# Sharing out the elementwise steps of the first MoE anew, and spreading the first row block of w3 x w_out2 over four heads

## The chip, the cores and the metric

The kernel runs on one core of one Trainium2 chip. The metric is the device time of one execution in microseconds. Before the change it is 1256.09 us, the median of three runs (1256.04 to 1257.05). The profile comes from a further execution of 1256.72 us.

The engines are TensorE (PE in the profile; PEld is its weight load), VectorE (DVE), ScalarE (ACT), GpSimd (POOL) and SyncE (SP), whose queue issues the loads and nearly all stores. Each engine takes its instructions in a fixed order, and one that waits holds up all behind it.

## The reference

Attention over 4 batches of 12 heads, sequence 448, head size 64, with q and k normalized; then two blocks of matrix products on 1792 tokens of width 768:

```
scores = (1/8) * rmsnorm(q, g_q) @ rmsnorm(k, g_k).T
x = softmax(scores) @ v                     # per head; then [1792, 768]
x = relu(x @ w_in)**2 @ w_out               # w_in 768x2048, w_out 2048x768
a, b = x @ w1, x @ w2                       # 768x1024 each
out = ((a * b) @ w3) @ w_out2               # w3 1024x1024, w_out2 1024x768
```

q, k and v are float32; the weights come as 64-bit floats.

## The kernel before

**Precision.** Nearly every product is made from three matmuls (`mm3`, L256 to L260): each float32 operand is held as a high half, rounded to the type that the PE takes (`F32R`), and a low half, the remainder. Making the halves of a tile is a copy (high, `copy_on`, L104/L106/L108 by engine) and a subtraction (low, `sub_on`, L112; its line is the same on DVE and POOL, so the profile tells them apart by engine and tile).

**Weights.** They come in units of 128x384 or 128x512, listed in `units` in the order of their use. Units 0 to 31 are w3 and w_out2, units 32 to 119 (`U0` to `U1`) are w_in, w_out, w1 and w2 for the first batch, all as 64-bit floats. Such a unit takes these steps: the load (L178, SP) into one of four 64-bit buffers; `words`, which turns the high word on ACT (L192) and the low word, called the conversion here, on ACT (L195) or POOL (L197); `join` on DVE (L204), which puts both together into one of four float32 buffers; the high half on ACT (L104); the low half on DVE or POOL (L112, tile `hl`). Units of the first batch's MoE are also stored as float32 (L212), and the later batches load those. A join frees the 64-bit buffer for the load four units on, and the low half frees the float32 buffer for the join four units on. `LOW_ENG` says by the unit's number modulo its length where the conversion runs (g POOL, a ACT), `LO0_ENG` the same for the low half of the first 120 units (v DVE).

**Stages.** `w3o` is w3 x w_out2, computed once: 8 row blocks (`ic`) of 16 groups of three matmuls, 384 matmuls in all (`gen_w3o`). The first block uses w_out2 for the first time, so each of its groups brings one more unit of w_out2 in; the later blocks find the 16 units in place. It runs beside heads 0 to 12. The MoE of batch b (`gen_moe`) runs beside the twelve heads of batch b + 1 and the last alone; it holds 336 groups of three matmuls, 28 a head. Within it, half of w_in (16 units), half of w_out (12), the other halves, w1 and w2 (32 units), then w3o (12 float32 units).

**Order.** The loop over heads (L663) traces the stages of a head, and between them six calls of `fill(n)`, each of which takes matmul groups from the running generator until their yields, 3 for a group, have used up the credit n. For w3o, n is the total `W3O` over 78 calls (13 heads). The tile framework's planner then fixes each engine's order at build time: it starts from the order of tracing and moves an instruction ahead where, by its own estimates, its inputs and buffers are there first. So the order on an engine is near that of tracing, not the same.

**Attention, as far as it is touched.** `head_prep` splits k and q; q's high half is scaled on the engine of `QHI_ENG` by batch (a ACT, L487; v DVE, L489), its low half on DVE. `stage_qk` makes scores (L520, L521) and their maxima (L522, tile `nb`), `stage_exp` the exponentials (L538, tile `p`), `stage_t` their transposes (L560, tile `pt`), whose halves go to `ptr`. `stage_v` multiplies by v (L609) into a PSUM bank of the pool `ps_kv`, which has one, and DVE adds the two parts (L617, tile `xf`). For each pair of heads `norms_to_rows` transposes the softmax sums (L598) into that same bank, and DVE multiplies `xf` by them (L623). The pool `ps_mm`, with three banks, serves the products of w3o and the MoE.

`relu2` (L324) follows each product of w_in: ACT makes the relu and its square's high half, DVE the square (L330, tile `gf`), POOL the low half (L112, tile `act`).

Of the kernel before, what the change touches and what calls it, by code (L numbers as in the profile page):

```python
# [8 lines left out]
F32 = mybir.dt.float32  # L9
# [20 lines left out]
def attention_moe_kernel(  # L30
# [25 lines left out]
    NIC = w3t.shape[0] // 2  # L56
# [3 lines left out]

    LOW_ENG = "gga"
    LO0_ENG = "ggggv"
    KHI_ENG = "ggvv"
    KLO_ENG = "gvvv"
    QHI_ENG = "aavv"
    VLO_ENG = "gvgv"


    SPLIT_AHEAD = 2
    HI_AHEAD = 1
    JOIN_AHEAD = 2
    WORD_AHEAD = 3
# [65 lines left out]
    U0 = len(units)  # L140
# [23 lines left out]
    U1 = U0 + 2 * NFC + 4 * NE + 4 * NJ  # L164
    raws = {}
# [23 lines left out]
    def words(i):  # L189
        t, n = raws[i], units[i][0].shape[-1]  # L190
        hi = t[:, :n, 1].bitcast(F32)
        nc.scalar.activation(out=hi, in_=hi, func=AF.Prelu, scale=2.0**-112, alpha=-(2.0**32))  # L192
        low = t.rearrange("p n t -> p (n t)").bitcast(U16).rearrange("p (n t) -> p n t", t=4)[:, :n, 1]
        if LOW_ENG[i % len(LOW_ENG)] == "a":
            nc.scalar.activation(out=t[:, :n, 0], in_=low, func=AF.Copy, scale=2.0**-13, bias=2.0**-14 - 0.5)  # L195
        else:
            nc.gpsimd.tensor_scalar(  # L197
                out=t[:, :n, 0], in0=low, scalar1=2.0**-13, scalar2=2.0**-14 - 0.5, op0=ALU.mult, op1=ALU.add
            )
# [26 lines left out]
    def split_lo(i):  # L226
        n = units[i][0].shape[-1]
        t = hls[i]
        sub_on(LO0_ENG[i % len(LO0_ENG)] if i < U1 else "g", t[:, 1, :n], raws.pop(i)[:, :n], t[:, 0, :n].bitcast(F32))

    def upto(what, i, step):
        while pos[what] <= min(i, NU - 1):
# [35 lines left out]
    def gen_w3o():  # L268
        for ic in range(NIC):
            ws = None  # L270
            for half in range(2):
                ps = ps_mm.tile([128, 512], F32, name="mm", tag="mm")
                for jc in range(NIC):
                    if ws is None or jc * 2 // NIC >= len(ws):
                        ws = (ws or []) + [use(w3_at[2 * ic + len(ws or [])])]
                    if ic == 0:
                        advance(wo_at[half, jc])
                        wo[half, jc] = hls.pop(wo_at[half, jc])
                    w = ws[jc * 2 // NIC]
                    mm3(ps[:, :HC], w, jc % (NIC // 2), hl_pair(wo[half, jc], HC), jc, NIC)  # L280
                    yield 3
                o = t2.tile([128, S], F32, name="osb", tag="osb")
                copy_on("a", o[:, :HC], ps[:, :HC])
                k, c = divmod(ic, NIC // 2)
                nc.sync.dma_start(
                    out=w3o.rearrange("(e k) p (c m) -> e k p c m", k=2, m=128)[half * 3:half * 3 + 3, k, :, c, :]
                    .rearrange("e p m -> p e m"),
                    in_=o[:, :HC].rearrange("p (e m) -> p e m", m=128),
                )
# [26 lines left out]
    def gen_moe(b):  # L316
# [4 lines left out]
        for half in range(2):  # L321
            g = []

            def relu2(ps):  # L324
                r = t2.tile([128, S], F32, name="r", tag="r")
                nc.scalar.activation(out=r, in_=ps, func=AF.Relu)
                t = actp.tile([128, 2, S], F32R, name="act", tag="act")
                gf = t2.tile([128, S], F32, name="gf", tag="gf")
                nc.scalar.activation(out=t[:, 0, :], in_=r, func=AF.Square)
                nc.vector.tensor_tensor(out=gf, in0=ps, in1=r, op=ALU.mult)  # L330
                sub_on("g", t[:, 1, :], gf, t[:, 0, :].bitcast(F32))
                g.append(t)

            def keep(e):
                def f(ps):
                    acc[e] = accp.tile([128, S], F32, name="acc", tag="acc")
                    copy_on("a", acc[e], ps)
                return f

            def add(e):  # L340
                def f(ps):
                    nc.vector.tensor_tensor(out=acc[e], in0=ps, in1=acc[e], op=ALU.add)
                    t = x2p.tile([128, 2, S], F32R, name="x2", tag="x2")
                    copy_on("v", t[:, 0, :], acc[e])
                    sub_on("g", t[:, 1, :], acc[e], t[:, 0, :].bitcast(F32))
                    x2[e] = t
                return f

            yield from products(u, x, KX, [relu2] * (NFC // 2), half == 0)
            u += NFC  # L350
            yield from products(u, g, KF, [(add if half else keep)(e) for e in range(NE)])
            u += 2 * NE
# [240 lines left out]
    def norms_to_rows(h):  # L593

        rs = sums2.pop(h // 2)
        ps = ps_kv.tile([128, 512], F32, name="kv", tag="kv")
        for c in range(C):
            nc.tensor.transpose(ps[:, c * P:(c + 1) * P], rs[:, c, :], ident)  # L598
        return ps[:, :S]
# [43 lines left out]
                state["gen"] = None  # L643

    MOE = 3 * (NFC * KX + 2 * NE * KF + 2 * NJ * KX + NE * NIC)
    W3O = 3 * 2 * NIC * NIC

    nc.sync.dma_start(out=g_sb, in_=g_in)
    load_group(0)
# [105 lines left out]
```

## Time and profile before

| | us |
|---|---|
| median of the runs | 1256.09 |
| the profiled execution | 1256.72 |
| its span, first to last instruction | 1254.9 |
| PE busy | 1176.6 (94%) |
| POOL busy | 788.5 (63%) |
| ACT busy | 749.0 (60%) |
| DVE busy | 692.6 (55%) |

The busy shares are means over stages of different kinds. In the page's forty slices of 31 us PE stands at 3, 7 and 8 tenths in the first three, at 9 in the next four, at 7 to 9, mostly 8, from the eighth to the thirteenth, which lie in the first MoE, and at 9 from there on. DMA is at 6 to 8 tenths in the first MoE and at 3 or 4 after it. So the stages are to be read one by one: by their busy time, then by what PE and DVE wait for in them.

### The profile page before, as it was taken

What the parts mean: (1) busy time and instruction counts of PE and PEld (TensorE: products, weight loads), DVE (VectorE), ACT (ScalarE), POOL (GpSimd) and SP (SyncE); (2) the same over time, 40 slices, a digit from 0 to 9 for tenths busy, and PEclk for the clock granted to TensorE, in tenths of its full rate; (3) what the DMA queues carried; (4) which work ended last, traced back from release to release, by engine and by line L of the source; (5) the groups of instructions that cost most, each with busy time, mean ns of one, the idle gap of its engine ahead of it and who ended that gap; (6) DMA issues with size and microseconds to landing.
All of it is one profiled execution on the core that took longest, in us unless ns stands there. A gap on an engine that the chain in (4) does not pass through costs nothing.

```text
span 1254.9 us, 18695 instructions
## 1 busy us (share of the span) xinstructions
PE 1176.6 (94%) x6192; PEld 1063.9 (85%) x6192; DVE 692.6 (55%) x1274; ACT 749.0 (60%) x1595; POOL 788.5 (63%) x770
## 2 busy tenths in 40 slices
PE   3789999798888999999999999999999999999998
PEld 2578888687777889999999998999999999999998
DVE  6699877666668676556557546555664431012100
ACT  5788877776755665665655555655545554443342
POOL 5874427746765555675876664765765656768773
PEclk9899999998998989999999999999999999999999
DMA  7774447866866754433334344333433333433342
GB/s 211 243 222 135 150 143 205 260 199 192 257 171 200 229 154 143 123 111 115 114 92 124 96 130 137 96 105 86 117 89 88 92 106 110 120 104 111 101 122 94
DMA packets 102129, 178.71 MB, mean 142 GB/s; under 512 B 11056, under 2 KB 65552, under 8 KB 102032
## 3 DMA queue, kind: packets, MB, share of 16 engines
q1 hardware_dynamic: 98576, 172.01, 46.9%
q10 hardware_dynamic: 3456, 5.51, 1.2%
q8 instruction: 49, 0.80, 0.3%
q14 instruction: 48, 0.39, 0.1%
HBM read 149.95 MB, written 27.53 MB: 141 GB/s over the span
## 4 chain that ended last, share of the span: by engine, by line
PE 65%; DVE 5%; DMA 4%; POOL 3%; ACT 2%; issue 2%; SPq 0%; POOLq 0%; DVEq 0%; ACTq 0%
PE mm L258 18%; PE mm L259 18%; PE mm L260 18%; PE pt L560 3%; PE kv L609 3%; DMA raw<-w 2%; DVE raw L204 2%; POOL hl L112 2%; PE sc L520 2%; PE sc L521 2%; DMA raw<-w_in 1%; DVE nb L522 1%; PE kv L504 1%; PE kv L598 1%; ACT p L538 0%
## 5 line engine op out<-in xcount | busy, mean ns | idle before, releaser
L112 POOL TENSOR_TENSOR hl<-raw,hl 128x384 fp32r<-128x384 f32 (+1 forms) x395 | 459.3, 1166 | 270.3 <-ACT hl L104 266.8
L104 ACT ACTIVATE hl<-raw 128x384 fp32r<-128x384 f32 (+1 forms) x416 | 234.0, 564 | 147.2 <-PE mm L260 79.3
L259 PE MATMUL mm<-x,hl 128*128 128x448 f32 (+1 forms) x832 | 307.3, 369 | 7.8 <-POOL x L112 7.8
L258 PE MATMUL mm<-x,hl 128*128 128x448 f32 (+1 forms) x832 | 311.9, 375 | 2.8 <-ACT x L104 1.8
L260 PE MATMUL mm<-x,hl 128*128 128x448 f32 (+1 forms) x832 | 306.3, 368 | 2.0 <-POOL hl L112 1.2
L258 PE MATMUL mm<-act,hl 128*128 128x448 f32 (+1 forms) x640 | 239.0, 373 | 0.0
L259 PE MATMUL mm<-act,hl 128*128 128x448 f32 (+1 forms) x640 | 235.7, 368 | 3.0 <-POOL act L112 2.9
L260 PE MATMUL mm<-act,hl 128*128 128x448 f32 (+1 forms) x640 | 234.6, 367 | 1.6 <-DVE hl L112 1.4
L538 ACT ACTIVATE p<-sc,nb,rr 112x448 f32<-112x448 f32 x192 | 137.5, 720 | 82.3 <-DVE nb L523 81.8
L259 PEld LDWEIGHTS mm<-x,hl 128*128 128x128 f32 x832 | 158.9, 191 | 21.7 <-POOL x L112 9.5
L258 PEld LDWEIGHTS mm<-x,hl 128*128 128x128 f32 x832 | 158.8, 191 | 17.4 <-ACT x L104 3.2
L260 PEld LDWEIGHTS mm<-x,hl 128*128 128x128 f32 x832 | 158.7, 191 | 16.3 <-POOL hl L112 2.3
L204 DVE SCALAR_TENSOR_TENSOR raw<-raw 128x384 uint32<-128x384 uint32 (+1 forms) x120 | 94.9, 794 | 77.0 <-POOL hl L112 66.3
L259 PEld LDWEIGHTS mm<-act,hl 128*128 128x128 f32 x640 | 121.9, 191 | 14.2 <-POOL act L112 4.6
L522 DVE TENSOR_REDUCE nb<-sc 112x1 f32<-112x448 f32 x192 | 113.3, 616 | 35.3 <-PE sc L521 34.0
L260 PEld LDWEIGHTS mm<-act,hl 128*128 128x128 f32 x640 | 121.8, 190 | 11.9 <-DVE hl L112 1.8
L112 POOL TENSOR_TENSOR act<-gf,act 128x448 fp32r<-128x448 f32 x96 | 117.5, 1225 | 22.0 <-DVE gf L330 8.5
L258 PEld LDWEIGHTS mm<-act,hl 128*128 128x128 f32 x640 | 122.2, 191 | 9.4
L112 DVE TENSOR_TENSOR ptr<-pt,ptr 128x448 fp32r<-128x448 f32 x144 | 86.8, 618 | 72.2 <-ACT ptr L104 72.0
L560 PE MATMUL pt<-ident,p 112*128 112x112 f32 (+1 forms) x768 | 101.0, 269 | 13.1 <-DVE ptr L112 10.3
L192 ACT ACTIVATE raw<-raw 128x384 f32<-128x384 f32 (+1 forms) x120 | 71.4, 598 | 57.9 <-DMA raw<-w 25.5
L560 PEld LDWEIGHTS pt<-ident,p 112*128 112x128 f32 (+1 forms) x768 | 82.5, 138 | 20.4 <-DVE ptr L112 10.9
(76 smaller groups left out, 1517.5 us busy)
## 6 DMA issues: line engine op xcount, KB each, us to landing
raw<-f_in SPq DMA_DIRECT2D x96, 192.0 KB, 2.4
raw<-f_out SPq DMA_DIRECT2D x72, 256.0 KB, 2.6
raw<-f SPq DMA_DIRECT2D x96, 192.0 KB, 2.4
raw<-w_in SPq DMA_DIRECT2D x32, 384.0 KB, 3.5
raw<-w_out SPq DMA_DIRECT2D x24, 512.0 KB, 4.2
raw<-w SPq DMA_DIRECT2D x32, 384.0 KB, 3.8
raw<-w3o SPq DMA_DIRECT2D x48, 256.0 KB, 2.7
qt<-q_t SPq DMA_DIRECT2D x48, 224.0 KB, 2.8
```

The costliest lines, as they stand in the source:

```text
L104: nc.scalar.activation(out=out, in_=in_, func=AF.Copy)
L112: e.tensor_tensor(out=out, in0=in0, in1=in1, op=ALU.subtract)
L192: nc.scalar.activation(out=hi, in_=hi, func=AF.Prelu, scale=2.0**-112, alpha=-(2.0**32))
L204: nc.vector.scalar_tensor_tensor(out=f[:, :n].bitcast(U32), in0=t[:, :n, 1], scalar=3, in1=t[:, :n, 0], op0=ALU.logical_shift_left, op1=AL ...
L258: nc.tensor.matmul(ps, w[:, 0, wk, :], x[0], start=(i == 0), stop=False)
L259: nc.tensor.matmul(ps, w[:, 0, wk, :], x[1], start=False, stop=False)
L260: nc.tensor.matmul(ps, w[:, 1, wk, :], x[0], start=False, stop=(i == last))
L520: nc.tensor.matmul(o[j], d["qh"][:, c * P:(c + 1) * P], d["kt"], start=True, stop=False)
L522: nc.vector.tensor_reduce(out=nb[:, j:j + 1], in_=o[j], axis=AX.X, op=ALU.max, negate=True)
L538: nc.scalar.activation(out=p, in_=o[j], func=AF.Exp, scale=d["rq"][:, c:c + 1], bias=nb[:, j:j + 1], accum_out=sm[:, i, c:c + 1],)
L560: nc.tensor.transpose(ps[:kn, c * P:(c + 1) * P], d["p"][c][:, k0:k0 + kn], ident)
L609: nc.tensor.matmul(ps[:, :S], w, m, start=(n == 0), stop=(n == len(ops) - 1))
```

## The change

Six edits:

- The conversions of units 32 to 119 all run on POOL; before, every third was on ACT.
- The low halves of units 32 to 119 run on DVE for every third unit (g, g, v); before for every fifth. Units 0 to 31 keep both patterns.
- q's high half of the second batch's heads (12 to 23) is made on DVE instead of ACT.
- In the first MoE alone, the low half of the squared relu is made on DVE instead of POOL.
- The first row block of w3o asks 10.5 credits for a group instead of 3 (`FIRST = 3.5`), and `W3O`, from which n follows, grows to match: 3 x 2 x 8 x (8 + 2.5) = 504 instead of 384.
- `norms_to_rows` takes its PSUM tile from `ps_mm` instead of `ps_kv`.

```diff
-    LOW_ENG = "gga"
-    LO0_ENG = "ggggv"
+    LOW_ENG = ("gga", "g")
+    LO_ENG = ("ggggv", "ggv")
...
-    QHI_ENG = "aavv"
+    QHI_ENG = "avvv"
...
+    FIRST = 3.5
...
-        if LOW_ENG[i % len(LOW_ENG)] == "a":
+        low_eng = LOW_ENG[i >= U0]
+        if low_eng[i % len(low_eng)] == "a":
...
-        sub_on(LO0_ENG[i % len(LO0_ENG)] if i < U1 else "g", t[:, 1, :n], raws.pop(i)[:, :n], t[:, 0, :n].bitcast(F32))
+        lo_eng = LO_ENG[i >= U0]
+        sub_on(lo_eng[i % len(lo_eng)] if i < U1 else "g", t[:, 1, :n], raws.pop(i)[:, :n], t[:, 0, :n].bitcast(F32))
...
-                    yield 3
+                    yield 3 * FIRST if ic == 0 else 3
...
-                sub_on("g", t[:, 1, :], gf, t[:, 0, :].bitcast(F32))
+                sub_on("g" if b else "v", t[:, 1, :], gf, t[:, 0, :].bitcast(F32))
...
-        ps = ps_kv.tile([128, 512], F32, name="kv", tag="kv")
+        ps = ps_mm.tile([128, 512], F32, name="mm", tag="mm")
...
-    W3O = 3 * 2 * NIC * NIC
+    W3O = 3 * 2 * NIC * (NIC + FIRST - 1)
```

## Rows read from the trace of the kernel before

**Rows 1.** Busy time by stretches: us, then each engine's busy time, clock, DMA.

```profile
12.85:57.70 44.85, 28.13 (x100) 20.08 (x100) 30.26 (x63) 29.90 (x65) 35.96 (x38) 0.92 0.73 230
57.70:190.90 133.20, 121.50 (x744) 109.36 (x743) 115.90 (x238) 113.03 (x245) 66.20 (x81) 1.00 0.55 164
213.30:467.30 254.00, 220.65 (x1087) 194.15 (x1088) 172.52 (x300) 169.08 (x364) 156.24 (x161) 0.93 0.71 210
535.20:735.80 200.60, 200.60 (x1088) 184.10 (x1087) 120.95 (x213) 116.93 (x254) 137.49 (x129) 1.00 0.38 111
```

**Rows 2.** The same view for L520 alone: PE and PEld, clock, DMA.

```profile
213.30:467.30 254.00, 14.69 (x36) 6.47 (x37) 0.93 0.71 210
535.20:735.80 200.60, 13.10 (x36) 6.25 (x36) 1.00 0.38 111
```

**Rows 3.** Waits of PE, 213.3 to 467.3: total us, times, longest.

```profile
PE kv L598 <- DVE xf L617: 11.9, 4, 4.2
PE pt L560 <- DVE ptr L112: 9.2, 5, 3.5
PE sc L520 <- ACT p L538: 8.8, 8, 2.9
```

**Rows 4.** Waits of DVE, 213.3 to 467.3.

```profile
DVE raw L204 <- POOL hl L112: 60.2, 36, 3.3
```

**Rows 5.** The chain of waits, 401 to 409: start, us, what.

```profile
401.84 3.39 DMA raw<-w
...
405.38 0.53 POOL raw L197
...
405.99 1.03 POOL hl L112
...
407.04 1.36 DVE raw L204
...
408.42 3.54 DMA raw<-w
```

**Rows 6.** POOL in order of time: first 512-wide conversion and first 512-wide low half.

```profile
307.86 0.85 POOL L197 TENSOR_SCALAR raw<-raw 128x512 uint32<-128x512 uint16 x1
...
327.87 1.29 POOL L112 TENSOR_TENSOR hl<-raw,hl 128x512 fp32r<-128x512 f32 x1
```

**Rows 7.** The chain's shares by line, 213.3 to 467.3.

```profile
by line: DMA raw<-w 11.5%; DVE raw L204 9.2%; POOL hl L112 8.5%; issue 7.8%; DMA raw<-w_in 5.5%; DVE nb L522 3.8%; PE mm L258 3.7%; PE mm L259 3.7%; PE mm L260 3.6%; ACT p L538 2.4%; POOL act L112 2.3%; ACT hl L104 2.2%; POOL raw L197 2.0%;
```

**Rows 8.** Groups by line and form, POOL and DVE, 213.3 to 467.3.

```profile
L112 POOL TENSOR_TENSOR act<-gf,act 128x448 fp32r<-128x448 f32 x20 | 24.6, 1231 | 15.7 <-ACT act L104 6.4 <-DVE gf L330 5.1 <-ACT act L329 3.8
L197 POOL TENSOR_SCALAR raw<-raw 128x384 uint32<-128x384 uint16 x32 | 20.6, 644 | 39.9 <-DMA raw<-w 20.0 <-DMA raw<-w_in 10.7 <-DVE nb L522 4.5
L197 POOL TENSOR_SCALAR raw<-raw 128x512 uint32<-128x512 uint16 x16 | 12.8, 801 | 3.2 <-DMA raw<-w_out 2.0
...
L112 DVE TENSOR_TENSOR hl<-raw,hl 128x384 fp32r<-128x384 f32 x11 | 7.7, 696 | 2.0 <-ACT hl L104 2.0
```

**Rows 9.** Groups by line and form, DVE, 500 to 1020.

```profile
L489 DVE TENSOR_SCALAR qh<-qt,gg 128x448 fp32r<-128x448 f32 x22 | 10.4, 475 | 0.0
```

**Rows 10.** Busy time of L259 alone, one matmul a group, 12.85 to 92.7.

```profile
12.85:92.70 79.85, 18.21 (x46) 9.55 (x46) 0.96 0.73 223
```

**Rows 11.** PE in order of time: the first score matmul of head 4.

```profile
89.32 0.46 PE L520 MATMUL sc<-kt,qh 128*112 128x448 f32 x1 [1.19 <-ACT p L538]
```

**Rows 12.** PE in order of time: the same matmul of two groups in succession.

```profile
66.69 0.33 PE L259 MATMUL mm<-x,hl 128*128 128x384 f32 x1
...
67.21 0.33 PE L259 MATMUL mm<-x,hl 128*128 128x384 f32 x1
```

**Rows 13.** Waits of PE, 12.85 to 57.7.

```profile
PE mm L259 <- POOL x L112: 7.5, 4, 2.9
PE mm L259 <- POOL act L112: 2.9, 4, 1.3
```

**Rows 14.** The join's line: count, duration in ns (least, median, most), forms.

```profile
L204 DVE SCALAR_TENSOR_TENSOR raw<-raw x120: 500/679/1637, 11.4 to 458.6; 128x384 uint32<-128x384 uint32 x80, 128x512 uint32<-128x512 uint32 x40
```

## The prediction

> **What bounds the kernel now.** I began with the busy time of each engine by stretches, cut at the first score matmul (L520) of a head [rows 1]. Two stretches hold the same TensorE work: heads 14 to 22, which run beside the first MoE, and the corresponding nine heads beside the second one; each has 36 L520 matmuls [rows 2] and about 1088 matmuls in all. The second takes 200.6 us with PE busy throughout, the first 254.0 us with PE busy for 220.6 us and a mean granted clock of 0.93 of full speed. So 53.4 us are lost there: 33.3 us in which PE stood still, and roughly 254.0 x 0.07 = 18 us of half clock. All that follows head 22 runs at PE's pace, so what is gained or lost before it reaches the end one for one. The other place with slack is the start: PE is busy for 28.1 of 44.9 us in heads 0 and 1, but for 121.5 of 133.2 us in the rest of the w3 x w_out2 stretch.
>
> Next came the waits of PE in the slow stretch [rows 3]: it waits for attention results that DVE is late with, hardly ever for a weight tile. DVE's own waits explain that [rows 4]: 60.2 us, in 36 pieces, before the join (L204), all for the POOL subtraction that makes the low half of an earlier weight unit (I call it LO) and by that gives the f32 buffer back. Everything queued on DVE behind the join stands too.
>
> Then the chain of waits, to see why POOL is late [rows 5]. One round there: load of a unit 3.39 us, its low-word conversion on POOL 0.53, LO 1.03, join 1.36, next load; 408.42 - 401.84 = 6.58 us. LO does not need the load before it; it only stands behind that unit's conversion in POOL's queue. The timeline shows how far ahead [rows 6]: the first 512-wide conversion (unit 76) runs at 307.86, and six 384-wide LOs, five on POOL and one on DVE, come between it and the first 512-wide LO at 327.87. So the conversion of unit i+6 stands ahead of LO(i). LO(i) frees the buffer of join(i+4), which frees that of load(i+8), whose conversion stands ahead of LO(i+2): two units a round, 3.29 us a unit. PE wants a 384-wide unit every 22.3 / 9.33 = 2.39 us (28 groups of three matmuls a head, three groups a unit; 22.3 is a ninth of 200.6). Where the conversion stands only five ahead, three units share a round, 2.19 us each, which is no limit. That is what limits this stretch.
>
> **The change, part by part.** The first MoE has 88 units, numbers 32 to 119.
>
> LO. Before, i%5 = 4 puts 18 on DVE and 70 on POOL. After, i%3 = 2 puts 30 on DVE: 24 leave POOL, 12 come to it. A join waits no longer for POOL where LO has left; I take the 60.2 us [rows 4] in proportion: -60.2 x 24/70 + 60.2 x 12/70 = -10.3 us. Bounds: -20.6 (those that come cost nothing) and the slower rival's +8.8.
>
> The relu-square subtractions, 16 in all, leave POOL for DVE. POOL act pieces make up 2.3% of the chain through the stretch [rows 7], 5.8 us for 20 instructions, 13 of them these (the rest are the gated ones): -3.8 us. Bounds 0 and 16 x 1.231 = -19.7 us [rows 8].
>
> What DVE takes in return: 12 net LOs and 16 subtractions at 0.696 us and 12 q conversions (heads 12 to 23) at 0.475 us (a row of the later batches, where DVE does them already): 8.4 + 11.1 + 5.7 = 25.2 us [rows 8, 9]. DVE's named pieces are 9.2 + 3.8 = 13% of the chain, smaller ones come on top; I take 20%: +5.0 us. Bounds 0 and +25.2. The new subtraction also makes DVE wait for ScalarE's square; nb, ptr and xf queue behind it, and PE waits for those. ScalarE is relieved, so I put nothing more on it.
>
> Conversions. 30 (i%3 = 2; 22 narrow, 8 wide) go from ScalarE to POOL: 22 x 0.644 + 8 x 0.801 = 20.6 us more there. They hold 2.0% of the chain now, 5.1 us for 48; 30 more: +3.2 us. Bounds 0 and +20.6. ScalarE's relief I cost at zero: its join-feeding work waits for loads in any case. After the change every unit's conversion stands in POOL's queue, but the units whose conversions move are the ones with LO on DVE (both i%3 = 2, and six is a multiple of three), so the six-ahead order closes on no LO that it did not close on before, except for the 12 that come.
>
> The bank. The norm transposes (L598) take one of three mm banks in place of the one kv bank, so they no longer wait for the xf add: 11.9 us in four spells [rows 3]. Neither the transposes nor the xf add are among the chain's larger pieces [rows 7]: PE would mostly run into the next late DVE result (ptr, in the same rows as the spells). I take an eighth, -1.4 us; bounds -11.9 and, as an mm bank is now held until DVE has multiplied by it (L623), 18 x 0.7 = +12.6 us if each of the 18 pairs of heads from the first MoE on held a product up for one DVE operation of 0.7 us.
>
> The start. The credit of the first row block goes from 48 to 168, the total from 384 to 504; a head gives 6/78 of the total, so the block takes 168/38.8 = 4.3 heads instead of 48/29.5 = 1.6. A third of the way through head 4 is 92.7 us (it begins at 89.32 [rows 11]); in the trace 46 of 128 groups had begun by then [rows 10], where the credits give 43. With 16 by then, 30 groups go later, each 0.52 us [rows 12]: 15.6 us of PE. The early heads lose the waits for unit halves, 7.5 + 2.9 = 10.4 us [rows 13], and the moved work as far as PE was the last engine there, its busy share 28.1/44.9 = 0.63: 9.8 us. The later heads gain 15.6 us. -10.4 - 9.8 + 15.6 = -4.6 us. Bounds: -22.1 (all 26.0 us saved early, and 11.7 us of PE's idle time later take the work in but for 3.9) and +5.2 (only the waits go). Next late in the early heads are ScalarE and DVE with softmax.
>
> Sum: -10.3 - 3.8 + 5.0 + 3.2 - 1.4 - 4.6 = -11.9 us. The profiled execution took 1256.7 us, of which 1254.9 are span and 1.8 lie around it; that makes 1244.8 for it, and its 0.6 us above the median of the runs, 1256.1, taken off, 1244.2.
>
> A rule that speaks against the change: some joins last far longer than the shortest, 0.500 us against 0.679 in the middle and 1.637 at most [rows 14]. The Trainium skill ("SBUF — State Buffer", section "Who interferes with whom") says that a VectorE instruction with two SBUF inputs and a GpSimd instruction that reads SBUF exclude each other for the whole of whichever began first. The trace agrees as far as that spread goes, and the moved subtractions are of that kind. What it would make of the sum, worked out from the rows, is the first rival.
>
> **Rivals.** *Port.* Each of the 28 moved subtractions is held up as the longest join was, 1.637 - 0.500 = 1.14 us: 31.9 us more on DVE, x 0.2 = +6.4, 1250.6 us. For it: the spread of the joins; against it: the LOs on DVE averaged 0.696 us in the same stretch. *Three units a round.* With POOL's queue shorter and a third of LOs off it, two-unit rounds become rare; half of the 53.4 us goes, with the start -31.3, 1224.8 us. For it: 3.29 against 2.19 us a unit; against it: the other two residues keep their conversion six ahead. *Slower.* The 12 LOs that come to POOL now stand behind a conversion that waits for its load, as DVE's did not. Each of the 8 narrow ones turns a three-unit round into a two-unit round, 3.29 - 2.19 = 1.10 us, +8.8, while the 24 that leave had conversions of ScalarE ahead of them, were in three-unit rounds, and bring nothing: 8.8 in place of -10.3, 1263.3 us. The other terms together are -1.6 us, so the time turns to the slower side where the LO term passes +1.6. For it: the rounds; against it: the 24 that leave also no longer stand behind POOL's other subtractions. *No change*, the LO term zero: 1254.5 us. That the block isn't spread, because the planner pulls matmuls ahead of their credit, would cost the 4.6 us of the start; 46 groups begun against 43 credited says that it follows the credits.
>
> **How the numbers follow.** Forecast 0.40, port 0.10, three units 0.19, no change 0.12, slower 0.19. Faster by over 0.2% (about 2.5 us, which is what a measurement here can tell from no change) is the first three, 0.69; same 0.12; slower 0.19. Since cases of both signs weigh, the range reaches from below the large gain, 1222, to the slower case, 1264; about 0.08 lies outside at either end. The forecast's own range is 1238 to 1250.
>
> **What would show it.** Heads 14 to 22 at 245 to 248 us with PE's clock above 0.93; DVE's wait for POOL before the join near 50 us; POOL about 12 us less busy in the first MoE and DVE about 25 us more; L598 no longer waiting for the xf add; head 4 reached before 89.3 us and head 13 some 5 us before 190.9. The prediction is wrong if that wait stays at 60 us or moves to another releaser, if conversions stand further ahead than six, or if the first thirteen heads take longer than before.

## The result, and the profile after

The kernel after takes 1263.87 us (median of 4 runs, 1263.61 to 1265.94) against 1256.57 for the kernel before on the same chip: ratio 1.0055, interval 1.0038 to 1.0071, about 7 us slower. The forecast was 11.9 us faster. The profiled execution has a span of 1261.8 us, 6.9 above that of before.

Busy time by stretches of the kernel after, cut at the same score matmuls and with the same columns as [rows 1]: heads 0 and 1, heads 2 to 12, heads 14 to 22, and the nine heads beside the second MoE.

```profile
12.10:49.90 37.80, 22.94 (x82) 16.22 (x83) 24.88 (x58) 26.16 (x58) 27.39 (x30) 1.00 0.73 222
49.90:201.90 152.00, 132.92 (x760) 119.91 (x759) 122.26 (x252) 113.73 (x248) 79.53 (x93) 0.92 0.52 154
224.50:473.80 249.30, 216.57 (x1087) 188.75 (x1088) 188.65 (x331) 152.11 (x330) 149.43 (x159) 0.97 0.72 213
541.70:743.20 201.50, 201.07 (x1088) 184.17 (x1087) 120.92 (x213) 116.61 (x254) 137.86 (x129) 1.00 0.39 110
```

Against [rows 1]: heads 0 and 1 are 7.1 us shorter, heads 2 to 12 are 18.8 us longer, heads 14 to 22 are 4.7 us shorter, the last stretch agrees to a microsecond. Head 13 begins at 201.9 instead of 190.9. So the loss arises in the first thirteen heads, where 4.6 us were to be gained, and the first MoE gives a part back. What it gives back is not idle time: PE stands still for 32.7 us in heads 14 to 22 (249.30 less 216.57) against 33.3 before. PE is busy for 4.1 us less with the same matmuls, at a granted clock of 0.97 instead of 0.93.

Waits of PE in heads 14 to 22 after:

```profile
PE pt L564 <- DVE ptr L114: 13.2, 8, 3.4
PE sc L524 <- ACT p L542: 6.3, 9, 1.5
PE mm L264 <- POOL hl L114: 4.6, 3, 2.9
```

and the first row of DVE's:

```profile
DVE raw L207 <- POOL hl L114: 49.4, 29, 3.8
```

The norm transposes' wait [rows 3] is gone and the one for `ptr` grew from 9.2 to 13.2 us. DVE's wait before the join fell from 60.2 [rows 4] to 49.4 us; 50 were forecast. DVE is 16.1 us busier there, POOL 6.8 us less.

Groups by line and form after, POOL and DVE in the same heads:

```profile
L200 POOL TENSOR_SCALAR raw<-raw 128x384 uint32<-128x384 uint16 x48 | 33.3, 694 | 42.9 <-DMA raw<-w 18.8 <-DMA raw<-w_in 10.8 <-DVE raw L207 6.4
...
L200 POOL TENSOR_SCALAR raw<-raw 128x512 uint32<-128x512 uint16 x23 | 21.7, 945 | 20.7 <-DMA raw<-w_out 15.8 <-DVE vhl L114 2.2 <-DVE khl L114 2.0
```

```profile
L114 DVE TENSOR_TENSOR hl<-raw,hl 128x384 fp32r<-128x384 f32 x17 | 12.6, 743 | 0.4 <-ACT hl L106 0.2
L114 DVE TENSOR_TENSOR act<-gf,act 128x448 fp32r<-128x448 f32 x13 | 10.0, 767 | 0.1
```

A narrow conversion takes 0.694 us instead of 0.644, a wide one 0.945 instead of 0.801 [rows 8], and a low half on DVE 0.743 instead of 0.696.

Now the start. The same matmul line in head 2, and, from a second window, in head 5 (count, duration in ns: least, median, most):

```profile
L263 PE MATMUL mm<-x,hl x3: 444/522/687, 53.1 to 63.4; 128*128 128x384 f32 x3
...
L263 PE MATMUL mm<-x,hl x5: 334/335/422, 98.7 to 101.7; 128*128 128x384 f32 x5
```

Waits of PE before head 4 after, for the low halves of w_out2's units:

```profile
PE mm L263 <- POOL x L114: 13.6, 5, 4.7
...
PE mm L263 <- POOL act L114: 3.4, 2, 2.0
```

These were 10.4 us before [rows 13], were to vanish, and are 17.0. The halves themselves come later. POOL's low halves of the w_out2 units in the tiles `x`, first before, then after (count, duration in ns, first and last start):

```profile
L112 POOL TENSOR_TENSOR x<-raw,x x7: 993/1217/1847, 15.7 to 54.7; 128x384 fp32r<-128x384 f32 x7
...
L114 POOL TENSOR_TENSOR x<-raw,x x7: 998/1377/1849, 14.5 to 77.3; 128x384 fp32r<-128x384 f32 x7
```

The last of them begins 22.6 us later: `gen_w3o` advances a unit of w_out2 together with the group that first uses it, so spreading the groups spread the making of the halves too. Last, two stretches side by side: up to head 4, and heads 6 to 12. Before:

```profile
12.85:89.30 76.45, 54.13 (x252) 42.73 (x252) 59.97 (x115) 56.30 (x121) 60.30 (x64) 0.96 0.72 218
...
112.30:190.90 78.60, 74.65 (x463) 68.22 (x464) 64.14 (x142) 66.08 (x146) 31.76 (x45) 1.00 0.48 142
```

After, with heads 2 and 3 by themselves as a third row:

```profile
12.10:85.70 73.60, 48.17 (x184) 36.65 (x185) 51.50 (x108) 49.70 (x109) 51.54 (x57) 0.86 0.64 194
...
108.00:201.90 93.90, 86.95 (x528) 80.57 (x529) 76.79 (x169) 71.77 (x156) 42.66 (x54) 0.98 0.50 146
...
50.00:85.70 35.70, 25.13 (x104) 20.33 (x103) 26.62 (x50) 23.43 (x52) 24.15 (x27) 0.71 0.54 162
```

Up to head 4 PE has 68 matmuls less and is busy for 6.0 us less, but it stands idle for 25.4 us against 22.3. Heads 6 to 12 hold 65 matmuls more and last 15.3 us longer.

### The profile page after: what moved, and what is told of

Same layout as the page of the kernel before. It is cut to its first block, busy times and chain, and to the rows that moved or that the text cites. A ratio compares the mean times of both kernels' runs of the same rounds, so it can differ in the third digit from the quotient of the medians.

```text
span 1261.8 us, 18712 instructions
## 1 busy us (share of the span) xinstructions
PE 1179.1 (93%) x6192; PEld 1065.9 (84%) x6192; DVE 710.9 (56%) x1314; ACT 727.8 (58%) x1553; POOL 784.4 (62%) x772
## 4 chain that ended last, share of the span: by engine, by line
PE 66%; DVE 9%; DMA 8%; POOL 7%; ACT 5%; issue 4%; SPq 0%; POOLq 0%; DVEq 0%; ACTq 0%
PE mm L263 18%; PE mm L264 18%; PE mm L262 18%; PE pt L564 4%; PE kv L613 3%; POOL hl L114 3%; DMA raw<-w 2%; PE sc L524 2%; PE sc L525 2%; DVE raw L207 2%; DMA raw<-w_out 2%; ACT p L542 2%; DVE nb L526 2%; DMA qn<-q_nat 1%; POOL raw L200 1%
## 5 line engine op out<-in xcount | busy, mean ns | idle before, releaser
L114 POOL TENSOR_TENSOR hl<-raw,hl 128x384 fp32r<-128x384 f32 (+1 forms) x383 | 445.4, 1166 | 269.0 <-ACT hl L106 266.1
L106 ACT ACTIVATE hl<-raw 128x384 fp32r<-128x384 f32 (+1 forms) x416 | 233.4, 564 | 145.5 <-PE mm L264 79.7
L200 POOL TENSOR_SCALAR raw<-raw 128x384 uint32<-128x384 uint16 (+1 forms) x110 | 83.9, 763 | 92.8 <-DMA raw<-w_in 23.6
L262 PEld LDWEIGHTS mm<-act,hl 128*128 128x128 f32 x640 | 122.1, 191 | 11.9 <-ACT acc L106 2.5
L264 PEld LDWEIGHTS mm<-act,hl 128*128 128x128 f32 x640 | 122.0, 191 | 11.2 <-POOL hl L114 1.7
L207 DVE SCALAR_TENSOR_TENSOR raw<-raw 128x384 uint32<-128x384 uint32 (+1 forms) x120 | 87.2, 731 | 59.7 <-POOL hl L114 54.5
L564 PE MATMUL pt<-ident,p 112*128 112x112 f32 (+1 forms) x768 | 100.6, 268 | 20.8 <-DVE ptr L114 20.6
## 6 DMA issues: line engine op xcount, KB each, us to landing
raw<-f_in SPq DMA_DIRECT2D x96, 192.0 KB, 2.4
raw<-f SPq DMA_DIRECT2D x96, 192.0 KB, 2.4
```

What stands on the lines that cost most here:

```text
L106: nc.scalar.activation(out=out, in_=in_, func=AF.Copy)
L114: e.tensor_tensor(out=out, in0=in0, in1=in1, op=ALU.subtract)
L200: nc.gpsimd.tensor_scalar(out=t[:, :n, 0], in0=low, scalar1=2.0**-13, scalar2=2.0**-14 - 0.5, op0=ALU.mult, op1=ALU.add)
L207: nc.vector.scalar_tensor_tensor(out=f[:, :n].bitcast(U32), in0=t[:, :n, 1], scalar=3, in1=t[:, :n, 0], op0=ALU.logical_shift_left, op1=AL ...
L262: nc.tensor.matmul(ps, w[:, 0, wk, :], x[0], start=(i == 0), stop=False)
L264: nc.tensor.matmul(ps, w[:, 1, wk, :], x[0], start=False, stop=(i == last))
```

## The experiments

Ratios are to the kernel before on the same chip; the us behind them are that ratio on 1256.6. "Before" or "after" says which kernel was edited. Times and waits inside a run come from one profiled execution of it.

**The first four: one part alone, or one undone.** After, with the block not spread:

```diff
-    FIRST = 3.5
+    FIRST = 1.0
```

> The changed kernel with the first row block's credit put back (FIRST = 1.0). Theory 1 (the credits cost the 11.0 us by which head 13 starts later, 201.9 against 190.9): head 13 starts near 191 us again, heads 14 to 22 keep about 249 us, time 1253 us, 3 to 4 us under the kernel before. Theory 2 (the norm transposes in the mm banks hold up the products of w3 x w_out2 at the start): head 13 stays near 200 us, time 1262 us. Theory 3 (the other engine shares make the planner order the start differently): as theory 2 here, told from it by the next runs.

1261.56 us, ratio 1.0026 (1.0012 to 1.0041), +3.3 us. The spread block alone does not explain the result: the rest is slower than before too. Theory 1 had head 13 near 191 us here; it begins at 201.5, as late as in the kernel after. Heads 6 to 12:

```profile
112.90:201.50 88.60, 79.25 (x460) 71.64 (x460) 70.90 (x150) 62.44 (x139) 35.94 (x48) 0.94 0.46 130
```

With no group moved they take 88.6 us instead of 78.6: PE is busy for 4.6 us longer with the same work, at a granted clock of 0.94 instead of 1.00, and stands still for 9.4 us instead of 4.0.

Before, with the spread block alone (the three lines with `FIRST` of the change):

> The kernel before with the credit of the first row block alone (FIRST = 3.5). Theory 1: head 13 starts near 202 us, heads 14 to 22 stay at 254 us, time 1267 us. Theories 2 and 3: head 13 near 191 us or, as the prediction had it, 186 us; time 1252 to 1256 us.

1268.47 us, ratio 1.0089 (1.0069 to 1.0109), +11.2 us. Head 13 begins at 198.1, 7.2 us late, and the first MoE is not better. From head 0 to head 6 it takes 91.6 us instead of 99.5, and from there to head 13, with 22 groups more, 93.6 instead of 78.6:

```profile
104.50:198.10 93.60, 87.19 (x526) 80.15 (x525) 76.30 (x165) 74.31 (x160) 39.96 (x50) 0.98 0.51 146
```

Before, with the bank alone:

```diff
-        ps = ps_kv.tile([128, 512], F32, name="kv", tag="kv")
+        ps = ps_mm.tile([128, 512], F32, name="mm", tag="mm")
```

> The kernel before with the norm transposes in an mm bank alone. Theory 1: no PE wait for the xf add any more, but another wait for DVE in its place; head 13 within 2 us of 191, heads 14 to 22 at 252 to 254 us; time 1254 to 1257 us. Theory 2: head 13 near 200 us, time 1265 us. Theory 3: as theory 1.

1262.6 us, ratio 1.0038 (1.0022 to 1.0055), +4.8 us, outside all three forecasts. Head 13 begins at 191.1 and heads 14 to 22 take 257.3 us. PE's longest waits in its heads 14 to 22:

```profile
PE pt L560 <- DVE ptr L112: 15.8, 7, 4.7
PE sc L520 <- ACT p L538: 10.5, 8, 3.2
PE mm L258 <- DVE gf L330: 5.0, 1, 5.0
```

The 11.9 us for the xf add [rows 3] are gone. In their place `ptr` and the exponentials are waited for 8.3 us longer, and a product itself waits 5.0 us for an mm bank that DVE has not read out yet.

Before, with the four elementwise edits alone (the first four of the change):

> The kernel before with the four edits of the elementwise steps and neither the credit nor the bank. Theory 1: head 13 within 2 us of 191, heads 14 to 22 at 249 to 251 us, time 1252 us. Theory 2: the same. Theory 3: head 13 near 200 us, time 1262 us.

1256.85 us, ratio 0.9989 (0.9979 to 1.0000), -1.4 us; -5.9 were forecast. DVE's wait before the join is 42.9 us, 17.3 less than before, and yet PE's idle time in heads 14 to 22 is 32.8 us, as before:

```profile
111.40:192.00 80.60, 74.75 (x463) 68.12 (x463) 68.21 (x151) 63.52 (x141) 35.28 (x48) 1.00 0.49 141
213.80:467.00 253.20, 220.43 (x1089) 193.63 (x1088) 190.53 (x331) 152.64 (x329) 147.93 (x159) 0.94 0.70 210
```

Head 13 begins at 192.0. So the bank alone and the elementwise edits alone leave the first thirteen heads nearly as they were, both together (the first run) delay them by 10.6 us, and none of the three theories holds by itself. Why the two together bring the lower clock and the idle time to heads 6 to 12 is not shown.

**Why the early heads kept their time.** The spread block alone, with 20 further small matmuls after each fill of heads 1 to 4, to keep TensorE's clock up:

```diff
         fill(n)
+        if 1 <= h <= 4:
+            junk(20)
```

> The kernel before with FIRST = 3.5 and, in heads 1 to 4, 20 additional 112-column matmuls of a constant after each fill, whose result nobody reads: they keep PE busy and cost it work, some 1 us a fill at full clock. With FIRST alone, heads 2 and 3 take 32.6 us (49.4 to 82.1) and PE's clock is at half for 13.6 us of heads 1 to 4. Theory 1 (with fewer matmuls the early heads run PE at half clock, and that eats what was taken off PE): the half-clock time falls to under 4 us and heads 2 and 3 get shorter, to 28 us or less, although PE has more to do. Theory 2 (POOL's queue sets the early heads: the low halves of w_out2 units stand behind the key preparation of later heads): heads 2 and 3 stay at 31 to 36 us whatever the clock. Theory 3 (the softmax chain of ScalarE and DVE sets them): as theory 2.

(The same two lines after each of the six fills of a head.) 1319.2 us, ratio 1.0485. The added matmuls cost far more than was thought, heads 2 and 3 took 52.4 us, outside all forecasts, and the clock in them still was 0.84 on average; this tells nothing of what the clock costs.

The spread block alone, with POOL relieved: k's halves and v's low half of heads 2 to 7 on DVE:

```diff
-        sub_on(KLO_ENG[h // H], khl[:, :, D:], kx, khl[:, :, :D].bitcast(F32))
+        sub_on("v" if 2 <= h < 8 else KLO_ENG[h // H], khl[:, :, D:], kx, khl[:, :, :D].bitcast(F32))
```

(k's high half and v's low half alike.)

> The kernel before with FIRST = 3.5 and, for heads 2 to 7, the key halves and v's low half on DVE instead of POOL: about 1.9 us a head less on POOL, 1.3 us more on DVE. Theory 2: PE's waits for unit halves from POOL (15.8 us before head 4 with FIRST alone) fall under 8 us and head 4 begins 5 us or more before 82.1. Theory 1: head 4 within 2 us of 82.1. Theory 3: head 4 at 84 us or later, as DVE has more to do.

1269.32 us, ratio 1.0089 (1.0064 to 1.0114). PE's waits before head 4 in the spread block alone:

```profile
PE mm L260 <- POOL x L113: 13.1, 6, 4.6
PE mm L260 <- POOL act L113: 2.7, 2, 1.4
```

and with POOL relieved:

```profile
PE mm L260 <- POOL x L113: 6.9, 5, 1.8
...
PE mm L260 <- POOL act L113: 2.2, 2, 1.5
```

6.7 us of waiting went, and head 4 began at 82.4 instead of 82.1, where theory 2 had it 5 us or more before.

The dose: the block spread over 8.2 heads, and over 2.9, instead of 4.3. Against the spread block alone:

```diff
-    FIRST = 3.5
+    FIRST = 12.0
```

> The kernel before with FIRST = 12: the first row block spreads over 8.2 of 13 heads, two groups a head, so the early heads are nearly attention alone. Theory 1: PE at half clock for most of heads 1 to 6, and these take 13 us or more each. Theories 2 and 3: heads 3 to 6 take 10 to 12 us each (the softmax chain's own pace), as POOL has fewer units to do in them. All: the later heads pay, head 13 begins after 215 us, time 1280 us or more; if it begins before 200 us the account by groups moved is wrong.

1275.88 us, ratio 1.0141 (1.0115 to 1.0167). By head 6, 17 groups have begun instead of 61, and head 6 comes only 11.1 us earlier; heads 6 to 12 take 104.4 us instead of 78.6. Head 13 begins at 205.7 and the time is below 1280 us, where all theories had over 215 and 1280 or more. Heads 3, 4 and 5 take 10.8, 13.2 and 13.4 us at granted clocks of 0.77, 0.87 and 0.75, which decides for neither side.

```diff
-    FIRST = 3.5
+    FIRST = 2.0
```

> The kernel before with FIRST = 2.0: the block spreads over 2.9 heads. With FIRST = 3.5 alone 22 groups moved past head 6; the early heads gained 7.8 us and the late ones paid 15.0. If the loss follows the groups moved (any of theories 1 to 3), about 10 groups move, the early heads gain 2 to 5 us, the late ones pay 6 to 8, time 1258 to 1262 us. If the loss with 3.5 is a chance of the planner's order, the time can lie anywhere between 1252 and 1270 us and head 13 does not follow the groups.

1259.35 us, ratio 1.0010 (1.0001 to 1.0020), +1.3 us, near the forecast for a loss that follows the groups moved: 8 moved past head 6, the heads before it gained 6.1 us (2 to 5 were expected) and heads 6 to 12 paid 7.1. With 22 groups it was 7.9 and 15.0 us, with 44 it was 10.7 and 25.8: what is saved grows far less with the groups than what is paid.

The spread block alone, where the first row block's third matmul takes w3's high half for its low half (`lo` is 0 in the first row block and 1 elsewhere):

```diff
-        nc.tensor.matmul(ps, w[:, 1, wk, :], x[0], start=False, stop=(i == last))
+        nc.tensor.matmul(ps, w[:, lo, wk, :], x[0], start=False, stop=(i == last))
...
```

> The kernel before with the spread block, in which the third matmul of each group of the first row block takes w3's high half instead of its low half: the same matmuls in number and size, the same steps on POOL, but PE no longer waits there for a low half that POOL is late with (15.8 us in all before head 4 with the spread block alone). The result of the first row block lacks the low half of w3. Theory 1: those waits set the pace of the early heads. Then head 4 begins near 68 us instead of 82.1, and the time falls from 1268.5 to about 1255 us. Theory 2: they are only where PE waits for a pace set by the rest of the chain and by the clock, as the run that took half of them away had it (6.7 us fewer waits, head 4 at 82.4): head 4 at 78 to 83 us, 1265 to 1270 us.

1266.7 us, ratio 1.0078 (1.0055 to 1.0101). This took the wrong half away: PE's waits sit at the second matmul, which reads w_out2's low half, and 13.2 us of them stayed. It decides nothing. The same with the second matmul:

```diff
-        nc.tensor.matmul(ps, w[:, 0, wk, :], x[1], start=False, stop=False)
+        nc.tensor.matmul(ps, w[:, 0, wk, :], x[lo], start=False, stop=False)
...
```

> The run before replaced the wrong half: PE's late low halves in the first row block are those of w_out2's units, the second matmul of a group, and it still waited 13.2 us for them. Here the spread block alone, with the second matmul of each group of the first row block on w_out2's high half instead of its low half: the same matmuls, the same steps on POOL, and no wait for a low half of w_out2 on PE in that block. Its result lacks the low half of w_out2. Theory 1: those waits set the pace of the early heads; head 4 begins near 68 us instead of 82.1, and the time falls from 1268.5 to about 1255 us. Theory 2: the pace is set elsewhere, as the run with half of the waits taken away had it: head 4 at 78 to 83 us, 1265 to 1270 us.

1265.6 us, ratio 1.0068 (1.0052 to 1.0083). PE's waits before head 4:

```profile
PE sc L521 <- ACT p L539: 5.9, 3, 5.1
PE kv L505 <- DVE xf L624: 2.9, 1, 2.9
...
PE pt L561 <- DVE ptr L113: 2.5, 3, 1.3
```

and the first rows of ScalarE's and of DVE's:

```profile
ACT p L539 <- DVE nb L524: 8.4, 2, 5.7
...
DVE nb L523 <- PE sc L522: 8.9, 7, 2.7
```

All 15.8 us of waiting for w_out2's low halves are gone, and head 4 begins at 79.7, 2.3 us earlier. Theory 2 stands: the pace is set elsewhere. PE now waits for exponentials, those for DVE's maxima, and those for PE's scores, but that is not all of it. In the chain of waits up to head 4,

```profile
by line: issue 15.7%; POOL hl L113 7.2%; PE pt L561 6.2%; POOL raw L198 5.8%; DVE nb L523 4.9%; POOL khl L113 4.3%; POOL khl L107 4.1%; PE kv L610 4.0%; POOL kx L477 3.7%; PE mm L261 3.4%; PE sc L521 2.7%; DVE ql L493 2.7%; DVE nb L524 2.6%
```

POOL's rows, for weight units and for the key preparation of later heads, add up to 25% and DVE's maxima to 7.5%. The windows up to head 4 of this kernel,

```profile
12.20:79.70 67.50, 46.50 (x184) 35.18 (x185) 51.55 (x108) 49.76 (x109) 52.77 (x56) 0.90 0.69 212
```

of the spread block alone,

```profile
12.90:82.10 69.20, 45.35 (x185) 34.05 (x186) 50.51 (x108) 48.60 (x107) 51.46 (x56) 0.90 0.65 199
```

and of the widest spread

```profile
12.40:74.60 62.20, 41.14 (x162) 30.02 (x163) 44.00 (x101) 42.09 (x95) 42.54 (x48) 0.89 0.59 177
```

give PE's idle time before head 4: 21.0, 23.9 and 21.1 us, beside 22.3 before and 25.4 after. Of each, 8.5 to 10.0 us lie in head 0. It depends little on how many groups are there or on what ends the waits.

**The first MoE, edit by edit.** After, with the norm transposes back in the kv bank:

> The kernel after with the norm transposes back in the kv bank; the four elementwise edits and the spread block stay. Theory A: the bank costs its 4.8 us in any company. Alone on the kernel before it gave 1262.6 against 1257.8 or so, and with the four elementwise edits 1261.6, which is their -1.4 us plus the same cost. Then this kernel takes 1263.9 - 4.8 = 1259.1 us, and heads 14 to 22 are some 3 us shorter than the 249.3 us of the kernel after. Theory B: the three edits share their gain and their loss with the spread block, the effects are not additive (singly -1.4, +10.9 and +4.8 make +14.3, together they made +7.3), and the bank costs nothing beside the spread block: -1.4 + 10.9 on 1256.6 gives 1266 us, with PE waiting for the xf add before the norm transposes again.

1264.12 us, ratio 1.0053 (1.0037 to 1.0068), as after. PE waits 12.0 us for the xf add before the norm transposes again, and beside the spread block the bank costs nothing: theory B, though its sum of single effects, 1266 us, is 2 us too high.

Before, with the units' low halves alone:

```diff
-    LO0_ENG = "ggggv"
+    LO_ENG = ("ggggv", "ggv")
...
```

> The kernel before with the low halves of every third unit of the first MoE on DVE instead of every fifth, and nothing else. Theory A, the prediction's own account: -10.3 us for the subtractions, and 12 more on DVE at 0.696 us and a fifth of it on the path, +1.7: 1248 us, with DVE's wait for POOL before the join near 50 us. The prediction's slower rival: +8.8 + 1.7, 1267 us. Theory B, from the run with all four edits (the wait fell from 60.2 to 42.9 us and the time by 1.4 us): what leaves the join goes into the next late result of DVE, and the time stays within 2.5 us of 1256.6.

1256.36 us, ratio 0.9988 (0.9973 to 1.0004), -1.5 us. DVE's wait before the join hardly moved from 60.2 us:

```profile
DVE raw L204 <- POOL hl L112: 59.6, 33, 3.6
```

Three elementwise edits, without the conversions:

> The kernel before with three of the elementwise edits: low halves of every third unit on DVE, the relu-square low half of the first MoE on DVE, and q's high half of the second batch on DVE; the conversions stay shared out 2 to 1 between POOL and ScalarE. Theory A: the 30 conversions that the fourth edit brings to POOL cost the 3.2 us that the prediction put on them; without them 1256.85 - 3.2 = 1253.6 us. Theory B: the stretch is set by DVE, which does the same here as with all four, and the time stays at 1256.9 within 1.5 us.

1249.65 us, ratio 0.9943 (0.9924 to 0.9963), -7.2 us: faster than both kernels. (Its profiled execution is its slowest, 1254.75 us.) DVE's wait:

```profile
DVE raw L204 <- POOL hl L112: 44.4, 26, 3.6
```

Before, with the conversions alone:

```diff
-    LOW_ENG = "gga"
+    LOW_ENG = ("gga", "g")
...
```

> The kernel before with all conversions of the first MoE's units on POOL, and nothing else. The four elementwise edits together took 1.4 us off, three of them without this one 7.2 us. Theory A: this edit has a price of its own, 1256.6 + 5.7 = 1262 us, as POOL's queue before the low halves grows by 30 instructions. Theory B: it costs only once the low halves have been shared out anew; alone it stays at 1256.6 within 1.5 us. The prediction's term was +3.2 us, 1259.8.

1268.76 us, ratio 1.0087 (1.0070 to 1.0104), +10.9 us, nearly twice what theory A gave. DVE's wait:

```profile
DVE raw L205 <- POOL hl L112: 65.4, 40, 3.2
```

and POOL's before the conversion:

```profile
POOL raw L198 <- DMA raw<-w: 25.7, 13, 4.7
...
POOL raw L198 <- DMA raw<-w_in: 14.4, 10, 2.3
...
POOL raw L198 <- DMA raw<-w_out: 2.9, 3, 1.6
```

POOL stands 43.0 us before conversions whose load has not landed, against 32.7 before [rows 8], with the low halves queued behind them. With the three edits in place it looks otherwise: there the conversions add 5.8 us of time while DVE's wait before the join goes from 44.4 to 42.9 us, and it is PE's wait for `ptr` that grows, three edits first, then four:

```profile
PE pt L561 <- DVE ptr L112: 5.9, 6, 1.8
...
PE pt L562 <- DVE ptr L112: 11.2, 6, 3.7
```

Before, with the relu-square low halves alone:

```diff
-                sub_on("g", t[:, 1, :], gf, t[:, 0, :].bitcast(F32))
+                sub_on("g" if b else "v", t[:, 1, :], gf, t[:, 0, :].bitcast(F32))
```

> The kernel before with the low half of the squared relu of the first MoE on DVE instead of POOL, and nothing else: 16 subtractions. The low halves of the units alone took 1.5 us off and three edits 7.2 us, so 5.7 us are left for this edit and q's high half. Theory A: this one frees POOL where the join waits for it, 1256.6 - 5.7 = 1251 us, with DVE's wait for POOL before the join below 50 us. Theory B: only the edits together do it, and this one alone stays within 2 us of 1256.6; the prediction's terms for it were -3.8 and 16 x 0.696 / 5 = +2.2, 1255.0.

1256.95 us, ratio 0.9993 (0.9978 to 1.0007), -0.9 us. DVE's wait is 57.0 us. Together with the units' low halves, without q's:

> The kernel before with the low halves of every third unit on DVE and the relu-square low halves of the first MoE on DVE; q's high half and the conversions as before. Singly these gave -1.5 and -0.9 us, and with q's high half -7.2 us. Theory A: the two need each other, since POOL must be relieved of both kinds before the join stops waiting for it: DVE's wait before the join falls to about 45 us, as with all three, and the time to 1250 us. Theory B: they add, and q's high half, which leaves ScalarE, brings the rest: DVE's wait near 57 us and 1254.2 us.

1252.63 us, ratio 0.9952 (0.9936 to 0.9968), -6.0 us, with

```profile
DVE raw L204 <- POOL hl L112: 45.3, 25, 3.6
```

Theory A: the two need each other. Singly they took 0.6 and 3.2 us off that wait, together 14.9. But heads 14 to 22,

```profile
213.30:462.70 249.40, 214.59 (x1089) 188.49 (x1088) 183.28 (x323) 167.51 (x361) 129.39 (x137) 0.97 0.70 213
```

hold 34.8 us of PE's idle time, no less than the 33.3 before. They are 4.6 us shorter because PE is busy for 6.1 us less, at 0.97 of full speed instead of 0.93.

After, with the conversions shared out as before:

```diff
-    LOW_ENG = ("gga", "g")
+    LOW_ENG = ("gga", "gga")
```

> The kernel after with the conversions shared out 2 to 1 between POOL and ScalarE as before. Theory A: the conversions cost the same 5.8 us in this company: 1263.9 - 5.8 = 1258.1 us. Theory B: their cost depends on the order that the planner finds and does not come back here: 1264 us within 2.

1258.3 us, ratio 1.0001 (0.9990 to 1.0012). Theory A: of the kernel after's loss this edit alone is 6.8 us by the ratios (5.6 by the medians), and its heads 14 to 22 take 242.6 us instead of 249.3. The same without the spread block:

> The kernel after without the spread block and with the conversions shared out as before: three elementwise edits and the bank. Without the bank it took 1249.65 us. Theory A: the bank costs its 4.8 us again, 1254.5 us. Theory B: the bank's cost came from the order that the planner finds and the stretch gains from it, as heads 14 to 22 do with the spread block (242.7 us with the bank and without the conversions, 247.5 without either): 1245 to 1249 us.

1254.94 us, ratio 0.9978 (0.9966 to 0.9990), -2.8 us. By the time theory A: against -7.2 without the bank, the bank costs 4.4 us here. The profiled executions (1253.13 us, and 1254.75 without the bank) do not show where: with the bank heads 14 to 22 are shorter, 244.7 us against 247.5, as theory B had it, and head 13 is 3.2 us longer.

## Why the prediction was wrong

The edits put on one after the other, against the forecast's terms:

| | forecast | measured | kernels |
|---|---|---|---|
| low halves, relu-square, q on DVE | -10.3 - 3.8 + 5.0 = -9.1 | -7.2 | three edits |
| conversions | +3.2 | +5.8 | three to four edits |
| bank | -1.4 | +4.6 | four edits to after with the block not spread |
| start | -4.6 | +3.6 | that to after |
| sum | -11.9 | +6.9 | |

All four erred to one side, by 1.9, 2.6, 6.0 and 8.2 us. The order matters: alone the start costs 11.2 us and the bank 4.8, and beside each other they cost less than their sum. Each difference is uncertain by 2 to 3 us.

**The start failed, and by its first two terms.** The late term was right as a mechanism. For 15.6 us, 30 groups were to move by a third of head 4; 21 did (25 had begun there, where the credits give 16). With the spread block alone 22 moved past head 6, and heads 6 to 12 became 15.0 us longer, 12.5 us of it PE's busy time, 0.57 us a group, the rest idle time. The kernel after shows 15.3 us there, but without its spread block they were 10.0 us longer already, so these are not the block's alone. The early terms, -10.4 for the waits and -9.8 for the work, gave 7.9 us by head 6 with the block alone, and 3.6 in the kernel after (99.5 us from head 0 to head 6, then 95.9). The step "the early heads lose the waits for unit halves" was false twice. The waits grew: the halves are made with the groups that use them and moved with them, the last from 54.7 to 77.3 us. And the wait was not the cause: with it taken away, 21.0 us of idle time stayed, where the five kernels above have 21 to 25. What sets that floor is not shown. Softmax, named as next late, has a part in it, since score, maximum and exponential wait for each other there, and so has POOL with a quarter of the chain. A part of the saved work came back by the clock as well: from 50 to 85.7 us after, 0.71 of full speed was granted on average, which is somewhat over half of the time at the lower level, and the same matmul took 0.522 us there instead of 0.335. How much of the floor is the clock is not settled either.

**The bank was mis-sized**, -1.4 (an eighth of 11.9 is 1.5) against +4.4 to +4.8 us in three companies. "PE would mostly run into the next late DVE result (ptr)" is what the trace of the bank alone shows. There an eighth of the wait as gain and nothing for the mm bank that is held was the wrong choice between -11.9 and +12.6: a product waited 5.0 us in one piece for the square to be read out of its bank. In the other two companies the profiled executions do not show it in heads 14 to 22, which became shorter in both: beside the four elementwise edits the loss lies in heads 6 to 12 (80.6 us, then 88.6), beside three it is not found. So the mechanism is shown for the bank alone only. Beside the spread block it costs nothing (+0.3); why is open.

**The conversions were mis-sized**, +3.2 against +5.8, within the bounds of 0 and 20.6. Their share of the chain counted only their own duration. For the conversions alone the price is POOL standing before a conversion whose load is late, with low halves behind it (32.7 to 43.0 us). With the three edits, where the 5.8 us were measured, DVE's wait before the join did not grow, and the way to the time is not shown. The account of rounds behind it was too simple: counted over the 88 units by start times, the conversion stands six ahead of the low half for 35, five ahead for 40, and after for 37 and 39. That it closes on no further low half held (four or fewer ahead: 8 units before, 9 after), but with a third of the conversions left on ScalarE it is 18 units with the three edits and 16 in the kernel after: the change gave up a looser queue that its other edits had brought. This link from order to time fits the runs and is not shown by one that changes the order alone.

**The three DVE edits** came out near the forecast as a sum, and not in its parts. The low halves in proportion, 24/70 of 60.2 us, was false: alone they left the wait at 59.6. False too was that the wait is worth its length, since "DVE's own waits explain that": the wait fell by 10.8 us in the kernel after and by 17.3 with the four edits, while PE's idle time there fell by 0.6 us in both; with three edits the wait fell by 15.8 and the idle time by 3.2. What these heads gained in the kernel after lies in PE's busy time, with 17.1 us at the lower clock instead of 34.1. Whether the shorter waits kept the clock up is not shown. The rival *Slower* gave 1263.3 us, nearly the time measured, but by the 12 low halves that come to POOL, and these edits are no loss in any run; the right number there was chance. *Port* fell by its size: the subtractions on DVE average 0.743 us (384 wide) and 0.767 (448 wide) against 0.696, not 1.14 us more. By the Trainium skill ("SBUF — State Buffer", section "Who interferes with whom") a VectorE instruction with two SBUF inputs contends with a GpSimd instruction that reads SBUF. The traces agree: of the 50 narrow joins in heads 14 to 22 before, the 32 that began with POOL idle took 0.554 us on average and the 18 that began beside a running POOL instruction 1.265; of the 17 narrow low halves on DVE after, 8 and 9 took 0.545 and 0.920. As only some meet one, the averages move little: the conversions on POOL became 8 and 18% longer, and the narrow joins shorter, 0.722 us after against 0.810. *Three units a round* and *no change* did not come: the wait fell to 49.4 us, as forecast, and the stretch by 4.7 us instead of 7.3, by the clock as said.

Of the signs named for a wrong prediction one spoke plainly: the first thirteen heads took longer, and head 13 came 11 us later, not 5 us earlier.

## What to carry to other kernels

A wait that ends last is not yet a cause: in both stretches here, where several engines wait for each other, PE's idle time stayed, or fell far less than the wait, when the wait was removed or shortened, so credit it only with what the next chain leaves. Work that is spread takes its preparation along if both are traced together. Work moved from such a stretch into one that PE bounds was paid in full where it arrived and saved in part where it left. And edits that pull on one queue are to be timed together and with one left out: two that bring 1 us each brought 6 together, and one at 6 to 11 us hid a gain of 7.

## What the runs showed that was not expected

TensorE's clock stood at its lower level (1.2 of 2.4 GHz) for 20.5 us of heads 2 and 3 after and never in the same heads before. With the spread block alone it was 13.7 us there, but it is not the block's doing only: with the units' low halves alone it was 17.1 us in head 1, with the relu-square ones alone 23.9 us in heads 1 and 2, against 6.8 us in head 1 before. And 20 small matmuls after each fill did not hold it up: with PE busy for 43.9 of 52.4 us the granted clock was still 0.84. And the effect of an edit depends on its company by as much as its size, the spread block between +3.6 and +11.2 us, the bank between +0.3 and +4.8, since the build-time order changes with each.
